# Block-sparse attention before two feed-forward layers: mask added on TensorE, one maximum per four heads, block keys apart

## The chip, the core and the metric

The kernel runs on one core of a Trainium2 chip. The core has five engines with queues of their own: TensorE (PE, matrix products into PSUM), VectorE (DVE), ScalarE (ACT), GpSimd (POOL) and SyncE (SP, which here only issues DMAs). The metric is device time in microseconds (us), the median of several runs.

## The reference

Attention over 2 batches of 8 heads, 768 positions and head size 64, then two feed-forward layers. A query sees the keys less than 16 positions away, and for each block of 32 keys one "block key" (the maximum over the block) and one "block value" (the mean), whose scores get log(32) on top:

```python
k_sum = k.reshape(B, H, nb, block, D).max(axis=3)        # block = 32, nb = 24
v_sum = v.reshape(B, H, nb, block, D).mean(axis=3)
scores_l = scale * np.matmul(q, k.transpose(0, 1, 3, 2)) # scale = 1/8
scores_s = scale * np.einsum('bhsd,bhnd->bhsn', q, k_sum) + np.log(block)
scores_l_m = np.where(mask_l, scores_l, -1000000000.0)   # |i - j| < 16
scores_all = np.concatenate([scores_l_m, scores_s], axis=-1)
a = np.exp(scores_all - np.max(scores_all, axis=-1, keepdims=True))
a = a / (np.sum(a, axis=-1, keepdims=True) + 1e-09)
out = np.matmul(a, np.concatenate([v, v_sum], axis=2))
x = moe(x):  h = x @ w_in;  (h - tanh(h)) @ w_out
y = moe2(x): h = x @ w_in;  (h * tanh(softplus(h))) @ w_out
```

The feed-forward layers have 1536 tokens, width 512 and inner width 2048.

## The kernel before

The attention works in 12 units u of 128 queries, six to a batch (UPB = 6). The eight heads are packed in four pairs hp; the two heads of a pair, e = 0 and 1, lie on partitions 0 to 63 and 64 to 127. The 128 queries of a unit fall in two halves s of T = 64, and a half sees a window of KW = 96 keys and NB = 24 block keys: KA = 120 columns of scores. So a score product uses a quarter (64 by 64) of TensorE's array, and four of them, for the two s and two e, can be in it at once.

For unit u the work is:

- **qk(u)** (L300): 16 float32 products of 120 columns. Each becomes two instructions in the trace. The tile kt of the unit holds the 160 window keys with a copy of the 24 block keys at either end, so that one run of 120 columns is window plus block keys. The results go to two PSUM tiles, "s" for e = 0 and "tr" for e = 1.
- **softmax(u, e)** (L316): for each of the four hp one fused DVE instruction adds the mask (a float32 tile, which also holds the log term), scales by -1/8, writes to the tile aa in SBUF and gives the minimum, which is the negated maximum. Four exponentials on ACT then turn aa into weights, with their sums.
- **norm(u)** (L334): the reciprocal of the sums on DVE, and one multiplication for each e, on POOL or (for the entries in NORM_DVE) on DVE.
- **a_trans(u, e)** (L346): four transposes on TensorE, and a copy asb from PSUM, on DVE for the entries in ASB_DVE and on ACT for the others.
- **av(u)** (L358): the products of weights and values, 32 instructions of 64 columns; then x_hi on ACT and x_lo on DVE (L369, L373) split the result in two for the feed-forward products.

The block keys come from k_sum (L250, a maximum on DVE for each of a batch's six key tiles); k_fill (L260) copies them to both ends of every kt. For the first batch load_k_own (L223) loads each unit's own 128 keys only, and k_edges (L228) copies the 16 edge keys from the neighbours on ACT. v_sum, v_trans and v_fill (L265 to L296) make the block values; v_trans(1) borrows a "tr" tile at step 17.

A loop of steps j (L439) writes the order out. At step j it issues qk(j/2) if j is even, softmax for (j-1), norm(u) at j = 2u+3, a_trans at j = 2u+5 and 2u+6, av at j = 2u+7, x_hi a step later, and then what the table `todo` (L383 to L431) has for that step: loads, k_sum, k_fill, v_sum. Each engine runs its queue in this order. Each PSUM tag has two buffers. From step 19 on, pieces of the feed-forward weights are converted in between (conv_tick), and at steps 24, 25 and 29 the first feed-forward products are put in TensorE's queue (more_in).

## Time and profile before

| | |
|---|---|
| time, median of 3 runs | 604.6 us (602.49 to 605.14) |
| the profiled execution: time, span | 603.07 us, 601.3 us |
| TensorE busy | 578.8 us, 96% of the span, 3212 instructions |
| DVE busy | 417.8 us, 69% |
| ACT busy | 328.5 us, 55% |
| POOL busy | 53.4 us, 9% |

A line of a timeline gives the start and the length in us, the engine, the line of the kernel, the operation, what it writes and reads, and, in brackets, how long the engine was idle just before and which engine's work ended that. The granted clock is 1.00 where TensorE runs at 2.4 GHz and 0.50 at 1.2 GHz.

### The profile page before, as it was taken

How to read it: one execution, taken by the hardware profiler on the slowest of the kernel's cores; microseconds unless marked ns; L12 is line 12 of the kernel's file. 1: busy time of each engine (PE TensorE's matmuls, PEld its weight loads, DVE VectorE, ACT ScalarE, POOL GpSimd, SP SyncE). 2: the span in 40 equal slices, each digit the busy share in tenths (PEclk: the TensorE clock that was granted, in tenths of full speed). 3: DMA queues.
4: the chain of work that ended last, by engine and by line, in shares of the span. 5: the costliest groups of instructions: out<-in, count | busy, mean ns of one | idle time of the engine just before them, and what ended most of it. 6: DMA issues, size and time to landing. Idle time of an engine off the chain costs nothing.

```text
span 601.3 us, 9203 instructions
## 1 busy us (share of the span) xinstructions
PE 578.8 (96%) x3212; PEld 479.0 (80%) x3212; DVE 417.8 (69%) x968; ACT 328.5 (55%) x791; POOL 53.4 (9%) x109
## 2 busy tenths in 40 slices
PE   6768899999999999999999999999999999999997
PEld 5556788888888888888888888888888888888885
DVE  5797978886251222377776489997688777597785
ACT  4788878885251122367765456664464444454442
POOL 6465660000000000000000000000000000000000
PEclk9798899999999999999999999999999999999999
DMA  9997567765020000226661102100100000100001
GB/s 271 257 306 213 154 184 238 222 218 168 0 88 0 1 0 1 62 88 192 197 186 43 40 8 63 52 2 1 55 16 1 1 1 0 71 1 1 1 1 70
DMA packets 32110, 52.20 MB, mean 87 GB/s; under 512 B 3200, under 2 KB 25728, under 8 KB 32064
## 3 DMA queue, kind: packets, MB, share of 16 engines
q1 hardware_dynamic: 32064, 51.62, 28.5%
q8 instruction: 25, 0.41, 0.3%
q14 instruction: 21, 0.17, 0.1%
HBM read 48.07 MB, written 3.15 MB: 85 GB/s over the span
## 4 chain that ended last, share of the span: by engine, by line
PE 88%; DMA 4%; DVE 3%; ACT 2%; SPq 1%; issue 1%; POOL 0%; ACTq 0%
PE aT L478 7%; PE aT L479 7%; PE tr L479 7%; PE x L479 7%; PE aT L480 7%; PE tr L480 7%; PE x L480 7%; PE x L478 7%; PE tr L478 7%; PE s L479 7%; PE s L478 7%; PE s L480 7%; DMA kt<-in_kw_dram 3%; ACT aa L329 1%; DMA vtc<-in_vt_dram 1%; PE x L363 1%
## 5 line engine op out<-in xcount | busy, mean ns | idle before, releaser
L503 DVE TENSOR_TENSOR glo<-t,ghi 128x512 fp32r<-128x512 f32 x48 | 33.4, 695 | 85.4 <-ACT ghi L498 85.4
L498 ACT ACTIVATE ghi<-t 128x512 fp32r<-128x512 f32 x48 | 30.2, 629 | 96.5 <-PE tr L480 96.5
L478 PE MATMUL aT<-xhi,w 128*128 128x512 f32 x192 | 74.9, 390 | 0.0
L478 PE MATMUL s<-xhi,w 128*128 128x512 f32 x192 | 74.9, 390 | 0.0
L480 PE MATMUL s<-xhi,w 128*128 128x512 f32 x192 | 74.7, 389 | 0.0
L480 PE MATMUL aT<-xhi,w 128*128 128x512 f32 x192 | 74.7, 389 | 0.0
L479 PE MATMUL s<-xlo,w 128*128 128x512 f32 x192 | 74.7, 389 | 0.0
L479 PE MATMUL aT<-xlo,w 128*128 128x512 f32 x192 | 74.7, 389 | 0.0
L114 ACT ACTIVATE top<-raw 128x256 f16<-128x256 bf16 x128 | 61.5, 486 | 12.2 <-ACT w L132 4.8
L121 DVE SCALAR_TENSOR_TENSOR cv<-raw,top 128x256 int32<-128x256 int32 x128 | 55.4, 434 | 11.8 <-ACT top L114 7.6
L132 ACT ACTIVATE w<-cv 128x256 fp32r<-128x256 f32 x120 | 47.6, 402 | 10.7 <-DVE cv L121 9.8
L137 DVE TENSOR_TENSOR w<-cv,w 128x256 fp32r<-128x256 f32 x114 | 48.4, 426 | 0.1
L534 DVE SCALAR_TENSOR_TENSOR t<-n,r 128x512 f32<-128x512 f32 x48 | 33.1, 689 | 17.4 <-ACT r L531 17.3
L503 DVE TENSOR_TENSOR glo<-n,ghi 128x512 fp32r<-128x512 f32 x48 | 33.1, 690 | 15.5 <-ACT ghi L498 15.5
L498 ACT ACTIVATE ghi<-n 128x512 fp32r<-128x512 f32 x48 | 30.3, 632 | 24.4 <-PE tr L479 16.1
L329 ACT ACTIVATE aa<-aa,neg 128x120 f32<-128x120 f32 x96 | 36.6, 384 | 12.4 <-DVE neg L324 12.4
L480 PEld LDWEIGHTS aT<-xhi,w 128*128 128x128 f32 x192 | 36.1, 188 | 7.5
L480 PEld LDWEIGHTS s<-xhi,w 128*128 128x128 f32 x192 | 36.1, 188 | 7.5
L478 PEld LDWEIGHTS aT<-xhi,w 128*128 128x128 f32 x192 | 36.0, 188 | 7.5
L478 PEld LDWEIGHTS s<-xhi,w 128*128 128x128 f32 x192 | 36.0, 188 | 7.5
L479 PEld LDWEIGHTS s<-xlo,w 128*128 128x128 f32 x192 | 36.0, 188 | 7.4
L479 PEld LDWEIGHTS aT<-xlo,w 128*128 128x128 f32 x192 | 36.0, 188 | 7.4
(97 smaller groups left out, 1293.1 us busy)
## 6 DMA issues: line engine op xcount, KB each, us to landing
raw<-in_w_dram SPq DMA_DIRECT2D x128, 255.8 KB, 3.6
vu<-in_vw_dram SPq DMA_DIRECT2D x24, 192.0 KB, 4.9
qt<-in_qt_dram SPq DMA_DIRECT2D x12, 256.0 KB, 4.9
vtc<-in_vt_dram SPq DMA_DIRECT2D x6, 512.0 KB, 6.7
out_dram<-o SPq DMA_DIRECT2D x9, 256.0 KB, 2.0
kt<-in_kw_dram SPq DMA_DIRECT2D x6, 320.0 KB, 8.5
kt<-in_kw_dram SPq DMA_DIRECT2D x6, 256.0 KB
out_dram<-t SPq DMA_DIRECT2D x3, 256.0 KB
```

Source lines behind the costliest of these rows:

```text
L114: nc.scalar.activation(out=tops[n % len(tops)].bitcast(F16).rearrange("p (n t) -> p n t", t=2)[:, :, 1], in_=raws[n].bitcast(BF16).rearran ...
L121: nc.vector.scalar_tensor_tensor(out=tmps[n], in0=raws.pop(n).bitcast(I32).rearrange("p (n t) -> p n t", t=2)[:, :, 0], scalar=13, in1=top ...
L132: nc.scalar.activation(out=hi, in_=t, func=ACTF.Copy)
L137: (nc.gpsimd if on_pool else nc.vector).tensor_tensor(out=W[i][:, 1, o:o + PW], in0=tmps.pop(n).bitcast(F32), in1=W[i][:, 0, o:o + PW].bit ...
L329: nc.scalar.activation(out=aa[u][:, e, hp, :], in_=aa[u][:, e, hp, :], func=ACTF.Exp, scale=-1.0, bias=neg[u][:, e, hp:hp + 1], accum_out= ...
L363: nc.tensor.matmul(out=xps[u][64 * e:64 * e + 64, hp, T * s:T * s + T], lhsT=vu[u % 3][:, s, 2 * hp + e, :], rhs=asb[u, e][:, hp, T * s:T ...
L478: nc.tensor.matmul(out=out, lhsT=w[0], rhs=x[0], start=first, stop=False)
L479: nc.tensor.matmul(out=out, lhsT=w[0], rhs=x[1], start=False, stop=False)
L480: nc.tensor.matmul(out=out, lhsT=w[1], rhs=x[0], start=False, stop=last)
L498: nc.scalar.activation(out=ghi, in_=t, func=ACTF.Copy)
L503: nc.vector.tensor_tensor(out=glo, in0=t, in1=ghi.bitcast(F32), op=ALU.subtract)
L534: nc.vector.scalar_tensor_tensor(out=ts[z], in0=ns[z], scalar=2.0, in1=rs[z], op0=ALU.add, op1=ALU.mult)
```

## The change

Four things change in the attention; the feed-forward layers stay.

1. qk(u) first puts the mask into PSUM: four bfloat16 products of an identity with the mask, repeated for the four hp (384 columns), and four of a constant matrix of ones with "logs" (96 columns), three rows of which add up to 8 log(32). Then, for each hp, four float32 products with the window keys (96 columns) and four with the block keys (24 columns) are added on top.
2. max_(u), at the odd step 2u+1, takes the maxima of four heads in one DVE reduction for each e, and one small multiplication makes the negated, scaled maxima of all eight. exps(u, e) reads the scores from PSUM.
3. The block keys stay in their own tensor ksum. k_fill and k_edges go, kt holds the 160 window keys alone, and all key loads bring their edges.
4. The tables for DVE go: norm multiplies on POOL always, a_trans copies on ACT for e = 0 and on DVE for e = 1. The block part of the values lies at the same partitions for both s, so a value load is one DMA and v_fill two.

```diff
-        kt = [kq.tile([128, HP, KU + 2 * NB], F32, name=f"kt{n}") for n in range(NK)]
+        kt = [kq.tile([128, HP, KU], F32, name=f"kt{n}") for n in range(NK)]
...
-        masks = [con.tile([128, KA], F32, name=f"mask{m}") for m in range(3)]
+        masks = [con.tile([128, KW], BF16, name=f"mask{m}") for m in range(3)]
+        logs = con.tile([128, NB], BF16, name="logs")
+        ones = con.tile([128, T], BF16, name="ones")
+        identb = con.tile([128, T], BF16, name="identb")
...
         def load_v(u):
-            for s in range(2):
-                nc.sync.dma_start(out=vu[u % 3][WND[s][0]:WND[s][1], s], in_=vw_d[u, s])
+            nc.sync.dma_start(out=vu[u % 3][NB:KA], in_=vw_d[u].rearrange("s p h d -> p s h d"))
...
-        def k_fill(u):
-            eng = nc.vector if u in FILL_DVE else nc.gpsimd
-            for o in (0, NB + KU):
-                eng.tensor_copy(kt[u % NK][:, :, o:o + NB], ksum[u // UPB])
...
         def qk(u):
+            w, b = u % UPB, u // UPB
             for e in range(2):
                 sc[u, e] = pst(("s", "tr")[e])[:, 0:HP * KA].rearrange("p (a n) -> p a n", a=HP)
-            for hp in range(HP):
+
+            def tiles(reg, lhs, rhs, first=False, last=False):
                 for s in range(2):
                     for e in range(2):
                         d = slice(64 * e, 64 * e + 64)
-                        k0 = s * (NB + T)
                         nc.tensor.matmul(
-                            out=sc[u, e][T * s:T * s + T, hp, :],
-                            lhsT=qt[u % 3][d, hp, T * s:T * s + T],
-                            rhs=kt[u % NK][d, hp, k0:k0 + KA],
+                            out=reg(sc[u, e][T * s:T * s + T]), lhsT=lhs(d, s), rhs=rhs(d, s),
+                            start=first, stop=last,
                         )
...
+            tiles(lambda z: z[:, :, NB:KA], lambda d, s: identb[d], mask, True)
+            tiles(
+                lambda z: z[:, :, 0:NB], lambda d, s: ones[d],
+                lambda d, s: logs[d].unsqueeze(1).to_broadcast([T, HP, NB]),
+            )
+            for hp in range(HP):
+                q = lambda d, s: qt[u % 3][d, hp, T * s:T * s + T]
+                tiles(lambda z: z[:, hp, NB:KA], q, lambda d, s: kt[u % NK][d, hp, T * s:T * s + KW])
+                tiles(lambda z: z[:, hp, 0:NB], q, lambda d, s: ksum[b][d, hp, :], False, hp == HP - 1)
+
+        def max_(u):
+            m = two.tile([128, 2, HP], F32, tag="max", name="max")
+            neg[u] = two.tile([128, 2, HP], F32, tag="neg", name="neg")
+            for e in range(2):
+                nc.vector.tensor_reduce(out=m[:, e], in_=sc[u, e], axis=AX.X, op=ALU.max)
+            nc.vector.tensor_scalar(
+                out=neg[u], in0=m, scalar1=-1.0 / math.sqrt(D), scalar2=None, op0=ALU.mult
+            )
...
-            for hp in range(HP):
-                nc.vector.tensor_tensor_reduce(
-                    out=aa[u][:, e, hp, :], in0=pv[:, hp, :], in1=m, scale=-1.0 / math.sqrt(D),
-                    scalar=3.0e38, op0=ALU.add, op1=ALU.min, accum_out=neg[u][:, e, hp:hp + 1],
-                )
             for hp in range(HP):
                 nc.scalar.activation(
-                    out=aa[u][:, e, hp, :], in_=aa[u][:, e, hp, :], func=ACTF.Exp,
-                    scale=-1.0, bias=neg[u][:, e, hp:hp + 1], accum_out=sums[u][:, e, hp:hp + 1],
+                    out=aa[u][:, e, hp, :], in_=pv[:, hp, :], func=ACTF.Exp,
+                    scale=1.0 / math.sqrt(D), bias=neg[u][:, e, hp:hp + 1],
+                    accum_out=sums[u][:, e, hp:hp + 1],
                 )
...
-                (nc.vector if 2 * u + e in NORM_DVE else nc.gpsimd).tensor_tensor(
+                nc.gpsimd.tensor_tensor(
...
-            if 2 * u + e in ASB_DVE:
+            if e:
                 nc.vector.tensor_copy(t, pv)
...
         for u in range(UPB):
-            load_k_own(u)
+            load_k(u)
...
+            if j < NJ and j % 2 == 1:
+                max_(j // 2)
             if 1 <= j <= NJ:
-                softmax(*divmod(j - 1, 2))
+                exps(*divmod(j - 1, 2))
```

**TensorE, the scores of unit 3 and what stands behind them.** Before (s_393 and tr_394 are the two score tiles, kt3 and qt0 the keys and queries, aT the transposes of unit 0, x the products with its values):

```order
L310 MATMUL s_393<-kt3_92,qt0_97 64x120
L310 MATMUL tr_394<-kt3_92,qt0_97 64x120
...
L349 MATMUL aT_419<-ident_106,aa_257 120x128 x4
L349 MATMUL aT_443<-ident_106,aa_300 120x128 x4
L363 MATMUL x_450<-asb_375,vu0_100 64x64
L363 MATMUL x_450<-asb_424,vu0_100 64x64
```

Now:

```order
L301 LDWEIGHTS identb_108
L301 MATMUL s_453<-mask1_104,identb_108 64x4x96
...
L301 LDWEIGHTS ones_107
L301 MATMUL s_453<-logs_106,ones_107 64x4x24
...
L301 MATMUL s_453<-kt3_92,qt0_97 64x96
...
L301 MATMUL s_453<-ksum_226,qt0_97 64x24
...
L356 MATMUL aT_499<-ident_109,aa_286 120x128 x4
L356 MATMUL aT_523<-ident_109,aa_347 120x128 x4
L370 MATMUL x_530<-asb_437,vu0_100 64x64
```

The 16 products of the unit have become 32 narrower ones, with eight bfloat16 products ahead of them; the transposes and the value products behind them are the same.

**DVE, from unit 8 to unit 9.** Before (rd: sums and reciprocals of unit 7, asb: copies of transposes, L324: the fused instruction with the row that stores its minimum, of unit 8 and then, from s_924, of unit 9):

```order
L336 TENSOR_SCALAR rd_877<-sums_782 128x8
L339 RECIPROCAL rd_877<-rd_877 128x8
L375 TENSOR_TENSOR xlo1_71<-x_804,xhi1_68 128x4x128
L353 COPY asb_888<-aT_883 120x512
L324 ISA aa_866,neg_867<-tr_833,mask1_104 128x120
L324 ISA neg_867 128x1
...
L353 COPY asb_955<-aT_950 120x512
L324 ISA aa_957,neg_958<-s_924,mask1_104 128x120
```

Now (max_1139 and neg_1140 are of unit 9, rd_1044 of unit 7, rd_1150 of unit 8):

```order
L343 TENSOR_SCALAR rd_1044<-sums_936 128x8
L346 RECIPROCAL rd_1044<-rd_1044 128x8
L382 TENSOR_TENSOR xlo1_71<-x_954,xhi1_68 128x4x128
L360 COPY asb_1137<-aT_1132 120x512
L324 TENSOR_REDUCE max_1139<-s_1086 128x4
L324 TENSOR_REDUCE max_1139<-tr_1087 128x4
L325 TENSOR_SCALAR neg_1140<-max_1139 128x8
L343 TENSOR_SCALAR rd_1150<-sums_1039 128x8
```

The maxima of both e of a unit now stand together, behind the copy asb that stood ahead of e = 0 alone, and one of the two copies has moved to ACT.

**ACT at the same place.** Before (aa_866 is unit 8, aa_957 unit 9, vu0 the transposed block values of v_trans(1)):

```order
L329 ACTIVATE aa_866,sums_868<-aa_866,neg_867 128x120 x4
L287 ACTIVATE vu0_100<-tr_890 24x512 x2
L371 ACTIVATE xhi1_68<-x_897 128x4x128
L329 ACTIVATE aa_866,sums_868<-aa_866,neg_867 128x120 x4
L329 ACTIVATE aa_957,sums_959<-aa_957,neg_958 128x120 x4
```

Now (aa_1038 is unit 8, aa_1144 unit 9):

```order
L335 ACTIVATE aa_1038,sums_1039<-s_979,neg_1034 128x120 x4
L362 ACTIVATE asb_1055<-aT_1050 120x512
L279 ACTIVATE vu0_100<-tr_1057 24x512 x2
L378 ACTIVATE xhi1_68<-x_1064 128x4x128
L335 ACTIVATE aa_1038,sums_1039<-tr_980,neg_1034 128x120 x4
L335 ACTIVATE aa_1144,sums_1145<-s_1086,neg_1140 128x120 x4
```

A copy of a transpose has come between the first four exponentials and vu, and the exponentials read the score tiles s and tr.

## Rows read from the trace of the kernel before

**Rows 1.** The page: busy time by engine, and shares of the last chain.

```profile
PE 578.8 (96%) x3212; PEld 479.0 (80%) x3212; DVE 417.8 (69%) x968; ACT 328.5 (55%) x791; POOL 53.4 (9%) x109
...
PE 88%; DMA 4%; DVE 3%; ACT 2%; SPq 1%; issue 1%; POOL 0%; ACTq 0%
```

**Rows 2.** Timeline of TensorE: start, length, work, idle time before.

```profile
62.11 1.15 PE L363 MATMUL x<-asb,vu 120*64 120x64 f32 x30 [1.65 <-DVE asb L353]
...
76.76 0.62 PE L349 MATMUL aT<-ident,aa 128*120 128x128 f32 x4 [0.16 <-POOL aa L341]
```

**Rows 3.** Timeline of ACT: first exponentials of units 2, 3, 5, 8, 9, 10.

```profile
19.18 0.40 ACT L329 ACTIVATE aa<-aa,neg 128x120 f32<-128x120 f32 x1 [0.38 <-DVE neg L324]
...
26.45 0.39 ACT L329 ACTIVATE aa<-aa,neg 128x120 f32<-128x120 f32 x1
...
35.86 0.39 ACT L329 ACTIVATE aa<-aa,neg 128x120 f32<-128x120 f32 x1 [0.86 <-DVE neg L324]
...
51.88 0.40 ACT L329 ACTIVATE aa<-aa,neg 128x120 f32<-128x120 f32 x1 [1.79 <-DVE neg L324]
...
57.31 0.40 ACT L329 ACTIVATE aa<-aa,neg 128x120 f32<-128x120 f32 x1 [0.59 <-DVE neg L324]
...
62.40 0.38 ACT L329 ACTIVATE aa<-aa,neg 128x120 f32<-128x120 f32 x1
```

**Rows 4.** Timeline of all engines at the start, unit 0.

```profile
8.79 0.69 DVE L255 TENSOR_REDUCE ksum<-kt 128x16 f32<-128x512 f32 x1 [0.18 <-DMA kt<-in_kw_dram]
...
9.82 0.28 PE L310 MATMUL s<-kt,qt 64*64 64x120 f32 x1 [2.31 <-DVE kt L263]
...
11.14 0.28 DVE L324 CUSTOM_DVE_ANT_0 aa<-s,mask 128x120 f32<-128x120 f32 x1 [0.59 <-PE tr L310]
...
11.47 0.40 ACT L329 ACTIVATE aa<-aa,neg 128x120 f32<-128x120 f32 x1 [2.44 <-DVE neg L324]
...
12.77 0.68 DVE L272 TENSOR_REDUCE vsum<-vtc 128x16 f32<-128x512 f32 x1
...
12.99 0.38 ACT L329 ACTIVATE aa<-aa,neg 128x120 f32<-128x120 f32 x1
```

**Rows 5.** A stretch (its last columns: clock, DMA share, GB/s), and POOL's timeline.

```profile
10.00:20.00 10.00, 6.54 (x102) 5.03 (x99) 8.31 (x55) 7.20 (x37) 6.10 (x15) 0.66 1.05 300
...
11.13 1.97 POOL L276 TENSOR_TENSOR vtc<-vtc 128x256 f32<-128x256 f32 x4 [2.94 <-DMA vtc<-in_vt_dram]
...
17.76 1.98 POOL L276 TENSOR_TENSOR vtc<-vtc 128x256 f32<-128x256 f32 x4 [0.56 <-DMA vtc<-in_vt_dram]
```

**Rows 6.** Timeline of DVE: two reductions in a row, one k_fill.

```profile
17.67 1.28 DVE L272 TENSOR_REDUCE vsum<-vtc 128x16 f32<-128x512 f32 x2
...
42.53 1.11 DVE L263 COPY kt<-ksum 128x96 f32<-128x96 f32 x2
```

**Rows 7.** Groups by form, 0 to 115 us: total busy us, mean ns of one.

```profile
L371 ACT ACTIVATE xhi<-x 128x512 fp32r<-128x512 f32 x12 | 7.0, 583 | 1.6 <-PE x L363 1.6
L498 ACT ACTIVATE ghi<-t 128x512 fp32r<-128x512 f32 x6 | 3.7, 617 | 0.0
```

**Rows 8.** Timeline of TensorE: scores, transposes, value products.

```profile
27.68 0.31 PE L310 MATMUL s<-kt,qt 64*64 64x120 f32 x1
...
28.66 1.09 PE L349 MATMUL aT<-ident,aa 128*120 128x128 f32 x8
...
30.59 1.15 PE L363 MATMUL x<-asb,vu 120*64 120x64 f32 x30 [0.58 <-ACT asb L355]
```

**Rows 9.** Timeline where v_trans(1) stands.

```profile
53.41 1.18 ACT L287 ACTIVATE vu<-tr 24x512 f32<-24x512 f32 x2
...
54.65 0.31 PE L310 MATMUL tr<-kt,qt 64*64 64x120 f32 x1 [1.18 <-ACT vu L287]
```

**Rows 10.** A normalising pair on POOL; TensorE's busy time and clock in a stretch.

```profile
58.30 1.94 POOL L341 TENSOR_TENSOR aa<-aa,rd 128x480 f32<-128x480 f32 x2 [3.06 <-PE x L363]
...
63.50:64.00 0.50, 0.50 (x18) 0.50 0.18 33
```

More of the change, by code (lines that the diff above doesn't have):

```diff
@@ L196, in constants @@
             make_identity(nc, ident)
-            k_edges(0)
+            for e in range(2):
+                h = slice(64 * e, 64 * e + 64)
+                nc.gpsimd.tensor_copy(identb[h], ident[h, h])
+            nc.gpsimd.memset(ones, 1.0)
+            nc.gpsimd.memset(logs, 0.0)
+            left = float(np.float32(math.sqrt(D) * math.log(BLK)))
+            for r in range(3):
+                part = float(np.float32(left).astype(mybir.dt.np(BF16)))
+                left -= part
+                for e in range(2):
+                    nc.gpsimd.affine_select(
+                        out=logs, in_=logs, pattern=[[0, NB]], base=-(64 * e + r), channel_multiplier=1,
+                        compare_op=ALU.not_equal, fill=part,
+                    )
+            assert left == 0.0
             for m in range(3):
                 nc.gpsimd.memset(masks[m], 0.0)
-                for s in range(2):
-                    rows = masks[m][T * s:T * s + T]
-                    nc.gpsimd.memset(rows[:, SUM[s][0]:SUM[s][1]], math.sqrt(D) * math.log(BLK))
-                    reg = rows[:, WND[s][0]:WND[s][1]]
+                for e in range(2):
+                    reg = masks[m][T * e:T * e + T]
                     conds = [([[1, KW]], -1, -1), ([[-1, KW]], 2 * WIN - 1, 1)]
-                    if (m, s) == (0, 0):
+                    if m == 0:
                         conds.append(([[1, KW]], -WIN, 0))
-                    if (m, s) == (2, 1):
+                    if m == 2:
                         conds.append(([[-1, KW]], KW - WIN - 1, 0))
@@ L253, in k_sum @@
                 ksum[b] = two.tile([128, HP, NB], F32, tag="ksum", name="ksum")
-            own = kt[u % NK][:, :, NB + WIN:NB + WIN + 128]
+            own = kt[u % NK][:, :, WIN:WIN + 128]
             nc.vector.tensor_reduce(
@@ L287, in v_trans @@
                 nc.scalar.activation(
-                    out=vu[0][SUM[s][0]:SUM[s][1], s].rearrange("p h d -> p (h d)"), in_=p[0:NB, :],
+                    out=vu[0][0:NB, s].rearrange("p h d -> p (h d)"), in_=p[0:NB, :],
                     func=ACTF.Copy, scale=1.0 / BLK,
@@ L292, in v_fill @@
         def v_fill(n):
[L293 to L296 removed]
+            nc.sync.dma_start(out=vu[n][0:NB], in_=vu[0][0:NB])
         sums, neg, aa, asb, xps, sc = {}, {}, {}, {}, {}, {}
         def qk(u):
+            w, b = u % UPB, u // UPB
             for e in range(2):
                 sc[u, e] = pst(("s", "tr")[e])[:, 0:HP * KA].rearrange("p (a n) -> p a n", a=HP)
[L305 removed]
+            def tiles(reg, lhs, rhs, first=False, last=False):
                 for s in range(2):
@@ new lines, in tiles, with mask @@
+                            start=first, stop=last,
+                        )
+            def mask(d, s):
+                m = masks[0 if (w, s) == (0, 0) else 2 if (w, s) == (UPB - 1, 1) else 1]
+                return m[d].unsqueeze(1).to_broadcast([T, HP, KW])
+            tiles(lambda z: z[:, :, NB:KA], lambda d, s: identb[d], mask, True)
[3 more added lines that the diff above has]
+            )
@@ L400, in attention @@
             k_sum(u)
-            if u:
-                k_edges(u)
-        for u in range(UPB):
-            if u == 0:
-                v_sum(0, 0, 1, True)
-            k_fill(u)
+        v_sum(0, 0, 1, True)
         for u in range(3, NU):
@@ L429, in attention @@
         at(17, L(v_fill, 1), L(v_fill, 2))
-        for u in range(7, 12):
-            at(2 * u - 3, L(k_fill, u))
         NJ = 2 * NU
```

37 lines of the change are left out of this document (7 added, 30 removed).

## The prediction

> **What bounds the kernel now.** The page comes first: TensorE is busy for 96% of the span and holds 88% of the chain that ended last [rows 1]. A share is an average over stages, so the next view is TensorE's own waits. At 62.11 us it has waited 1.65 us for a copy on DVE, and from there to the end its only visible wait is one of 0.16 us at 76.76 [rows 2]. Whatever the attention stage gains or loses before the products av(7) at 62.11 moves the end one for one, and so does work added to TensorE after it; the two feed-forward layers do the same work in both kernels. The question is when av(7) starts.
>
> Before that no single engine is the bound. I follow the first exponentials of each unit (128 queries) on ACT: units 5 and 10 begin theirs at 35.86 and 62.40, so a unit takes 26.54 / 5 = 5.31 us [rows 3]. TensorE's own share of a unit is about 0.98 us of scores, 1.09 of transposes and 1.15 of products with the values [rows 8], 3.2 us. The rest is waiting in a ring: scores, maxima on DVE, exponentials on ACT, normalising on POOL, transposes, copies.
>
> **Start.** The first six key blocks now come with their edges, 320 KB each instead of 256, so 384 KB more stand ahead of everything. In the window 10 to 20 us the queue moves 300 GB/s and the DMA share is full [rows 5]: 1.3 us later. The low end is 0, if whole rows of 2.5 KB move faster than 512-byte pieces; no row shows that, so I take 1.3. The ten edge copies on ACT go and free nothing here, since ACT waits then. The new constants lie on POOL, which is idle for 2.94 us before its first sum [rows 5]; they cost nothing as long as they take no more than that on top of what is there, and their excess if they do. On SP the value loads and the fills of vu are half as many; the keys of the second batch stand behind them there, so this can only help, and I count nothing. The last block's maximum starts at 8.79 us [rows 4]; 1.3 later, and with the maxima below, unit 0's exponentials fall behind 11.47 by some 2.4 us. Part of that is absorbed: unit 2's maxima stand behind the value sums on DVE, whose last input lands at 17.76 [rows 5], then at 19.05. From there one block sum 0.7, maxima 1.4 and 0.1 of waiting give 21.2 us for unit 2's exponentials, against 19.18 [rows 3].
>
> **Scores on TensorE.** Today 32 instructions of 120 columns take 27.68 to 28.66, 0.98 us, 31 ns each with four quarter arrays at work [rows 8]. The change replaces them with 32 of 96 columns, by columns 0.78 us, 32 of 24 columns, and eight bfloat16 products of 384 and 96 columns. The 24-column ones cost 0.20 us by columns. Their high end is the pace of the value products, 30 of 64 columns in 1.15 us on two half arrays [rows 8], 38 ns each, 1.2 us; halved, because four quarters work at once, it is 0.6. I take 0.4, the middle of 0.20 and 0.6. No row shows a bfloat16 product: four of 384 columns and four of 96 at today's rate per column make 0.49 us, the low end is 0 if TensorE does them while it waits for keys or queries, and I take 0.25. Together 1.43 us, with ends 0.98 and 2.5. The Trainium skill, TensorEngine Tiling (Array Packing), section Instruction Overhead, speaks against the split: it says that a matmul has some 60 cycles of overhead and that one column takes as long as sixty. By that rule the 24-column products would cost 0.49 us at 60 columns each instead of 0.4, a pass 1.52 us, and the end 0.5 us more, 606.3 us; no row here has so narrow a product, so the trace neither agrees nor disagrees.
>
> **Maxima on DVE.** What goes: eight fused mask-and-minimum instructions, 11.14 to 12.77, 1.63 us a unit [rows 4], but the first of them released ACT after 0.33 us. Also the copies of the block keys into kt, about 1.1 us for a unit's pair beside busy POOL [rows 6]. What comes: two reductions of 480 elements and one small multiplication. Two reductions of 512 take 1.28 us [rows 6]; from PSUM I take 1.2 for both and 0.2 for the rest, 1.4 us (ends 1.3 and 1.6). So DVE's work falls, but all eight exponentials of a unit wait for the whole 1.4 us. From start of scores to first exponential the path was 9.82 to 11.47, 1.65 us [rows 4]; it becomes 1.43, 0.25 for the last product's own time, and 1.4: 3.1 us.
>
> **Exponentials.** Four take 11.47 to 12.99, 1.52 us [rows 4]. They now read PSUM; a 512-wide ACT copy costs 583 ns from there and 617 from SBUF [rows 7], so 34 ns less each, 1.4 us for four (ends 1.25 and 1.55).
>
> **The new ring.** The score tiles stay in PSUM until ACT has read them; so far DVE freed them. Scores of unit u+2 wait for the last exponentials of unit u. On TensorE's queue a transpose stands behind those scores; on DVE the copy of that transpose stands ahead of the maxima. Two units therefore take: scores 1.7 with the last product, transpose 0.55, copy 0.7, maxima 1.4, then on ACT 1.4, copy 0.5, x_hi 0.5, 1.4. That is 8.15 us, 8.75 with a block sum in DVE's queue: 4.1 to 4.4 a unit. I take 4.3 against 5.31.
>
> **Where v_trans stands** the ring breaks. There the scores wait for ACT to read the transposed sums out of the same pair of tiles: today vu at 53.41 lasts 1.18 us, scores follow at 54.65 [rows 9], and unit 8 to unit 9 takes 51.88 to 57.31, 5.43 us [rows 3]. The change puts a transpose copy, 0.5, before vu on ACT: 1.4 + 0.5 + 1.2 + 1.7 + 0.55 + 0.7 + 1.4 = 7.45 us. At unit 2 to 3 the same, with a block sum and some slow clock, is 8.2 us, against 7.27 [rows 3]; the key blocks then land no later than they are asked for.
>
> **The sum.** First exponentials: unit 2 at 21.2, unit 3 at 29.4, unit 5 two rings later at 38.0 (35.86, so 2.1 late), unit 8 at 50.9 (51.88, 1.0 early), unit 9 at 58.4 (57.31, 1.1 late), unit 10 at 63.1 with a weight conversion of 0.4 (62.40, 0.7 late). av(7) came 0.3 us ahead of that last time; now the maxima lie between, so it comes 1.4 ahead: 61.7, 0.4 early. After it, unit 11's scores cost 0.45 more, and normalising the last two units stands whole on POOL, 1.94 us for two halves [rows 10], about 1.0 us of it more than now and all counted. The copies of the transposes alternate (12 on ACT, 12 on DVE, where it was 13 and 11), which the ring's terms hold. The granted clock was half in 63.5 to 64 [rows 10], behind the wait of 1.65 us; a shorter wait could spare up to 1.7 us there, and the longer one at unit 9 could cost as much, so I put 0. In all -0.4 + 0.45 + 1.0 = +1.1 us. The profiled execution took 603.07 us, 1.8 more than its span of 601.3; the median is 604.6. On the median: 605.7, say 605.8 us.
>
> **Rivals.** (a) Faster: columns alone set TensorE's pace, scores 0.98 us. That takes 0.45 from each of two v_trans steps and from unit 11, 0.22 from each of the six ring steps between units 3 and 10, 2.7 us; the half clock goes too, 1.7. 605.8 - 4.4 = 601.4. For it: today's scores keep four quarters busy at 31 ns. Against it: the value products keep 38 ns at half the columns. (b) Slower: narrow products do not overlap four at a time and the scores take 2.5 us: 1.07 more in two v_trans steps and unit 11, 0.53 in six ring steps, 6.4 us: 612.2. It decides from about 1.75 us a pass, where the loss passes 3 us. (c) The change does not do what it says: DVE gets free time, but ACT's waits for it stay, since the eight exponentials hang on one instruction. Then a unit keeps 5.3 us, the six ring steps give nothing, 6.0 us lost: 611.8. Against it: the second four exponentials need no further wait.
>
> **How the numbers follow.** About 0.5% (3 us) is what a measurement of this kernel can tell from no change. The forecast, a small loss within that, has 0.46; (a) has 0.20; (b) and (c) together 0.34. The low end 601.0 takes (a) in; the high end 612.0 stops just short of (b) and (c), and leaves out what may lie beyond.
>
> **What would show it.** Unit 2 at about 21 us, units apart by 4.3 where 5.31 stood, 7 us or more from unit 8 to unit 9, score passes of 1.4 us, and no TensorE wait worth naming after av(7). A pass of 1.0 or of 2 us, or unit 9's first exponentials before 57 us, would prove the sum wrong.

## The result, and the profile of the changed kernel

The changed kernel takes 608.13 us (median of 9 runs, 606.36 to 610.59), the kernel before 603.29 us in the same session (9 runs, 601.87 to 605.14): 1.0083 times as long, with a 95% interval of 1.0061 to 1.0104. That is 4.8 us more where 1.2 were forecast (605.8 on 604.6), inside the range, but four times the size, and past the 0.5% that can be told from no change.

The profiled execution of the changed kernel is the longest of the nine: 610.59 us, with a span of 608.8, against 603.07 and 601.3 before. Its trace shows 7.5 us of loss, 2.7 more than the medians. The page, which answers [rows 1]:

```profile
PE 585.1 (96%) x3692; PEld 486.2 (80%) x3692; DVE 407.9 (67%) x791; ACT 322.3 (53%) x780; POOL 55.8 (9%) x111
...
PE 89%; DVE 4%; ACT 3%; DMA 1%; issue 1%; POOL 0%; SPq 0%; ACTq 0%
```

DVE and ACT have less to do, as the change intended, and TensorE has 480 products more, with as many weight loads. The shares say nothing about where the time went. The timeline of ACT does: the first exponentials of units 2, 3, 5, 8, 9 and 10, which answer [rows 3].

```profile
21.54 0.36 ACT L335 ACTIVATE aa<-s,neg 128x120 f32<-128x120 f32 x1 [1.57 <-DVE rd L343]
...
30.98 0.36 ACT L335 ACTIVATE aa<-s,neg 128x120 f32<-128x120 f32 x1 [5.22 <-DVE rd L343]
...
39.72 0.36 ACT L335 ACTIVATE aa<-s,neg 128x120 f32<-128x120 f32 x1 [0.26 <-DVE neg L325]
...
56.33 0.36 ACT L335 ACTIVATE aa<-s,neg 128x120 f32<-128x120 f32 x1 [2.98 <-DVE rd L343]
...
65.19 0.36 ACT L335 ACTIVATE aa<-s,neg 128x120 f32<-128x120 f32 x1 [4.15 <-DVE rd L343]
...
70.05 0.36 ACT L335 ACTIVATE aa<-s,neg 128x120 f32<-128x120 f32 x1 [0.37 <-DVE rd L343]
```

| step, us | before | forecast | changed kernel | over forecast |
|---|---|---|---|---|
| start to unit 2 | 19.18 | 21.2 | 21.54 | 0.3 |
| unit 2 to 3 (v_trans) | 7.27 | 8.2 | 9.44 | 1.2 |
| units 3 to 5 | 9.41 | 8.6 | 8.74 | 0.1 |
| units 5 to 8 | 16.02 | 12.9 | 16.61 | 3.7 |
| unit 8 to 9 (v_trans) | 5.43 | 7.45 | 8.86 | 1.4 |
| unit 9 to 10 | 5.09 | 4.7 | 4.86 | 0.2 |

The six excesses make 6.9 us: unit 10 at 70.05 where 63.1 was forecast. On TensorE the main part of av(7), which answers the first of [rows 2], starts 6.5 us late:

```profile
68.65 1.15 PE L370 MATMUL x<-asb,vu 120*64 120x64 f32 x30 [0.47 <-DVE asb L360]
```

The end is 7.5 us late, so what lies behind av(7) costs 1.0 us (1.45 forecast). What the forecast missed lies before av(7), mostly in two places: from unit 5 to unit 8, and in the two steps with v_trans. Against the kernel before, units 5 to 8 lose only 0.6 us; what is missing there is the 3.1 us that were to be gained, which should have paid for the start and the v_trans steps.

**Units 5 to 8.** The timeline of TensorE stops twice in the middle of a score pass:

```profile
43.98 0.24 PE L301 MATMUL tr<-ksum,qt 64*64 64x24 f32 x2
45.62 0.18 PE L301 MATMUL s<-ksum,qt 64*64 64x24 f32 x1 [1.39 <-issue]
...
49.89 0.24 PE L301 MATMUL s<-ksum,qt 64*64 64x24 f32 x2
52.11 0.18 PE L301 MATMUL tr<-ksum,qt 64*64 64x24 f32 x1 [1.97 <-issue]
```

"issue" means that nothing in the profile held the engine. All that these products need was there: their neighbours of the same pass, with the same keys and queries, had run. The kernel before has no such wait. That leaves the instructions themselves. They come by DMA queues of their own; TensorE's, by its packets, in the kernel before and in the changed one:

```profile
q8 instruction: 25, 0.41, 0.3%
```

```profile
q8 instruction: 29, 0.48, 0.3%
```

TensorE's 2 x 3692 products and weight loads over 29 packets are 255 to a packet, 2 x 3212 over 25 are 257: the queue brings pages of some 256 instructions. The trace also has each of these packets, 16384 bytes long, with its time: one runs from 42.96 to 44.30 and the next from 49.42 to 50.69, and the two waits end 1.3 and 1.4 us behind their ends. With the few semaphore instructions of TensorE's queue counted, it stops after 1473 and after 1729 instructions of the program: 256 apart.

A unit had 144 of them (64 for the scores, 16 for the transposes, 64 for the products with values); now it has 224. One page lasted 1.8 units, some 9 us; now it lasts 1.1, under 5 us in a ring of 4.3. Meanwhile the DMA engines are full with loads: a share of 1.02 in both of these stretches, in which TensorE does next to nothing (columns as in [rows 5]). That a page stands behind the loads is the theory to test.

```profile
44.00:45.50 1.50, 0.22 (x11) 0.12 (x4) 1.21 (x3) 1.50 (x9) 1.42 (x4) 1.00 1.02 386
50.00:52.00 2.00, 0.13 (x6) 0.03 (x1) 0.28 (x1) 2.00 (x9) 2.00 (x3) 1.00 1.02 197
```

**The v_trans steps.** TensorE waits for vu longer than in the kernel before, where it was 1.12 us (at 21.94) and 1.18:

```profile
24.47 0.48 PE L301 MATMUL tr<-mask,identb 64*64 64x384 bf16 x1 [1.79 <-ACT vu L279]
...
59.27 0.48 PE L301 MATMUL tr<-mask,identb 64*64 64x384 bf16 x1 [2.58 <-ACT vu L279]
```

Behind these waits the granted clock is half:

```profile
24.50:27.00 2.50, 2.50 (x71) 2.50 (x70) 0.00 (x0) 1.27 (x8) 0.00 (x0) 0.50 0.41 109
...
59.50:61.50 2.00, 2.00 (x65) 2.00 (x61) 0.00 (x0) 1.54 (x9) 0.00 (x0) 0.50 0.52 131
```

The pass from 59.27 takes 2.7 us where one at full clock takes 1.5, and the eight transposes behind it 1.96 instead of 1.09. The kernel before is not free of this: its eight transposes at 23.43 took 1.96 us as well, and over 10 to 75 us the mean granted clock is 0.87 in both traces. So the half clock is a cost against the forecast, which had these steps at nearly full clock; over the whole attention these two traces have the same share of it.

**At the start** a third thing was not foreseen. Without the edge copies, ACT's first work is an exponential, and the load of its table, which ran at 0.73 before anything was needed, now stands right ahead of it:

```profile
13.07 1.28 ACT L335 ACT_TABLE_LOAD   x1 [13.07 <-DVE neg L325]
14.37 0.36 ACT L335 ACTIVATE aa<-s,neg 128x120 f32<-128x120 f32 x1
```

### The profile page after: what moved, and what is told of

Its sections match the earlier page's. It is cut to its first block, busy times and chain, and to the rows that moved or that the text cites. A ratio compares the mean times of both kernels' runs of the same rounds, so it can differ in the third digit from the quotient of the medians.

```text
span 608.8 us, 9955 instructions
## 1 busy us (share of the span) xinstructions
PE 585.1 (96%) x3692; PEld 486.2 (80%) x3692; DVE 407.9 (67%) x791; ACT 322.3 (53%) x780; POOL 55.8 (9%) x111
## 4 chain that ended last, share of the span: by engine, by line
PE 89%; DVE 4%; ACT 3%; DMA 1%; issue 1%; POOL 0%; SPq 0%; ACTq 0%
PE aT L480 7%; PE x L480 7%; PE tr L480 7%; PE aT L482 7%; PE aT L481 7%; PE tr L482 7%; PE x L482 7%; PE x L481 7%; PE tr L481 7%; PE s L480 7%; PE s L482 7%; PE s L481 7%; ACT aa L335 2%; DVE max L324 2%; PE s L301 1%; PE aT L356 1%
## 5 line engine op out<-in xcount | busy, mean ns | idle before, releaser
L521 ACT ACTIVATE t<-aT 128x512 f32<-128x512 f32 x24 | 14.4, 599 | 44.2 <-PE aT L482 30.7
```

Of the source, the lines that this page charges most:

```text
L521: nc.scalar.activation(out=t, in_=hs[z], func=ACTF.Exp)
```

## The experiments

The theory: the narrow products make TensorE run out of instructions while the DMA engines are full ("fetch"), and the steps with v_trans lose time to the half clock behind the longer waits for vu. The rivals: the waits come from the products themselves or from PSUM; the table load or the wait of all eight exponentials is what counts. Ratios are to the kernel before, run beside each; the interval of the changed kernel itself is 1.0061 to 1.0104. e1_table and e2_merged lie above it, e7_before_more and e13_fill_act below; the times of the others cannot be told from it, and there the traces decide, each of one execution.

### The table load: e1_table and e5_table64

```diff
     nc.gpsimd.memset(two_c, 2.0)
+    early = big.tile([128, 1], F32, name="early")
+    nc.scalar.activation(out=early, in_=two_c, func=ACTF.Exp)
```

> One tiny exponential on ACT is put ahead of everything, so that the table load (1.28 us at 13.07 in the changed kernel, right ahead of unit 0's first exponential) happens while ACT is idle. If that load lies on the path that sets the end, unit 0's exponentials start at 13.0 instead of 14.37, unit 2's at 20.3 to 20.6 instead of 21.54, and the time falls by 0.6 to 1.3 us, to about 607.0. If the value sums or the loads bound unit 2 anyway, unit 2 moves by less than 0.4 us and the time stays within 0.3 us of 608.1.

619.19 us, ratio 1.0262 (1.0240 to 1.0284): 11 us more instead of 1 less. The load did move to 0.73 and unit 0 to 13.01. But in the stretch 120 to 600 us, far from the edit, fewer products fit (the number behind TensorE's busy time). The same stretch of e1_table, then of e5_table64:

```profile
120.00:600.00 480.00, 480.00 (x2077) 389.87 (x2077) 317.63 (x598) 235.20 (x468) 0.56 (x2) 1.00 0.17 51
```

```profile
120.00:600.00 480.00, 480.00 (x2119) 397.59 (x2118) 323.37 (x606) 237.90 (x469) 0.56 (x2) 1.00 0.16 50
```

e5_table64 differs in one number, `big.tile([128, 64], ...)[:, 0:1]`.

> The early exponential of e1_table again, but its result takes the first column of a tile of 64 columns (256 bytes) instead of a tile of 1 column, so that the tiles allocated behind it (weights, activations) move by 256 bytes and not by 4. If e1_table lost its 11 us because the products of the feed-forward layers read tiles that are shifted by 4 bytes (395 ns each instead of 389), they are back at 389 ns here and the time is 606.5 to 607.8: 608.1 less what the table load costs on the path. If the early exponential itself is to blame, the time stays near 619.

608.77 us, ratio 1.0080 (1.0052 to 1.0108). So the 11 us of e1_table came from the 4 bytes by which its tile moved all tiles behind it. With 256 bytes the products are back at full pace; in the trace unit 0's exponentials start at 12.71 and unit 2's at 20.18, 1.36 us earlier than in the changed kernel. Unit 5 keeps this gain (38.35, 1.37 earlier), and the span of the trace is 605.6, 3.2 us shorter; the medians of eight and nine executions show nothing of it (608.77 and 608.13). So the table load is on the path of the first units, but no gain from taking it away can be seen in the time.

### Fewer instructions with wider weights: e2_merged

```diff
-                tiles(lambda z: z[:, hp, 0:NB], q, lambda d, s: ksum[b][d, hp, :], False, hp == HP - 1)
+                both(
+                    lambda z: z[:, hp, 0:NB], lambda d: qt[u % 3][d, hp, :],
+                    lambda d: ksum[b][d, hp, :], False, hp == HP - 1,
+                )
```

(`both` makes one product for e = 0 and one for e = 1, with 128 columns of weights; logs and inner masks likewise. A pass of the inner units has 104 instructions, not the 100 of the expectation.)

> The products with the block keys, with logs and (in the eight inner units) with the mask are made for both halves of a unit by one instruction with 128 columns of weights: a score pass has 100 instructions (weight loads and products) instead of 144. Theory 'fetch': TensorE stands still at 43.98 and 49.89, in the middle of a pass, because it has run through a page of 256 instructions before the next page came in. With 40 instructions less in a unit both waits vanish, unit 6 to unit 8 takes 9 to 10 us instead of 12.5, and the time falls by 3 to 5 us, to 603 to 605. Rival 'something else holds a pass up in its middle' (PSUM, the products of the block keys themselves): waits of 1 to 2 us within a pass stay, and only the shorter pass is gained, 0.1 to 0.3 us a step: 606.5 to 608.

626.41 us, ratio 1.0382 (1.0362 to 1.0402). The waits in the middle of passes are gone (one wait for instructions is left, 0.73 us at 63.16, between transposes), but a pass now takes 3.08 us at full clock (41.85 to 44.93) instead of 1.44. TensorE's timeline, one group of keys and one of block keys, and the next (first and last of each):

```profile
42.28 0.29 PE L302 MATMUL s<-kt,qt 64*64 64x96 f32 x1
...
42.61 0.29 PE L314 MATMUL s<-ksum,qt 64*128 64x24 f32 x1
...
42.75 0.27 PE L314 MATMUL tr<-ksum,qt 64*128 64x24 f32 x1
42.95 0.29 PE L302 MATMUL s<-kt,qt 64*64 64x96 f32 x1
```

Four instructions of 24 columns take 0.34 us of the queue (42.61 to 42.95), as much as eight of 96 (0.33): a group of one form (64 by 64) does not overlap with one of the other (64 by 128). The Trainium skill, TensorEngine Tiling (Array Packing), section Key Properties, says that a change of the tiling mode drains TensorE; this trace agrees, 0.33 us per group, eight times in a pass. The run answers its question only half: instructions were saved, but at a slower pace a page lasts longer anyway.

### More instructions in the kernel before: e7_before_more

```diff
+            for n in range(20):
+                for e in range(2):
+                    d = slice(64 * e, 64 * e + 64)
+                    nc.tensor.matmul(out=sc[u, e][0:T, 0, 0:1], lhsT=tiny[d, 0:T], rhs=tiny[d, 0:1])
             for hp in range(HP):
```

> The kernel before, with 40 bfloat16 products of one column (80 instructions with their weight loads) put ahead of the scores of each unit on TensorE; the scores then overwrite their result. Theory 'fetch': with 80 instructions more a unit runs through about a page, as in the changed kernel, and waits that the trace cannot put down to another engine, 0.5 to 2 us long and some 256 instructions apart, appear on TensorE between 35 and 60 us, where the kernel before has none. Rival 'the waits come from the products of the block keys or from the mask': no such wait here; the time grows only by what the tiny products take, 0.5 to 1.5 us in a pass.

605.71 us, ratio 1.0037 (1.0014 to 1.0059), and the waits appear, four of them, in a kernel that had none:

```profile
17.52 0.36 PE L316 MATMUL s<-kt,qt 64*64 64x120 f32 x1 [1.47 <-issue]
...
37.46 0.16 PE L310 MATMUL s<-tiny 64*64 64x1 bf16 x1 [0.75 <-issue]
...
43.67 0.16 PE L310 MATMUL s<-tiny 64*64 64x1 bf16 x1 [1.50 <-issue]
...
49.90 0.16 PE L310 MATMUL s<-tiny 64*64 64x1 bf16 x1 [0.60 <-issue]
```

The last three come 2, 16 and 30 tiny products into a unit's pass: each time 14 products, 28 instructions, further on, and a unit has 224; 252 from one wait to the next, and 256, a page, with the four semaphore instructions in between. From 37.46 to 43.67 and to 49.90 are 6.2 us each. The rival falls: neither mask nor block keys are needed for such a wait, only the count. The place in the program says the same: in the eleven traces of this document that have such waits, 23 in all, TensorE stops each time 193 or 194 instructions behind a multiple of 256, whatever product stands there, and goes on 1.3 to 1.8 us after the end of a packet of its instruction queue.

### Fewer transfers: e3_raw_late and e11_quiet

```diff
-        at(12, L(v_sum, 1, 0, 1, True), L(conv_ahead, n_raw))
+        at(12, L(v_sum, 1, 0, 1, True))
...
-        at(16, L(v_sum, 1, 2, 1))
+        at(16, L(v_sum, 1, 2, 1), L(conv_ahead, n_raw))
```

> The first loads of raw weights, six of 256 KB, are issued at step 16 instead of step 12; nothing else changes. Theory 'the page of instructions stands behind the data in the DMA engines': in 43 to 53 us there is less to move, the waits of 1.39 and 1.97 us in the middle of passes shrink to under half or vanish, and the time falls by 1 to 3 us, to 605 to 607. Rival 'a page takes the same time whatever else moves': both waits stay at 1.4 and 2 us, and the time is 608 or, as the weights then come late, more.

607.16 us, ratio 1.0055 (1.0034 to 1.0076). The two waits are 0.62 and 1.43 us, and a third one of 1.15 us has come at 63.53, where the late loads now run (DMA share 0.64 in 62 to 64, where the changed kernel has 0.00). The waits go where the transfers go, but their sum stays (3.20 us; 3.36 in the changed kernel).

e11_quiet moves these loads to step 18 and leaves the three loads of the second batch's values for v_sum out:

```diff
         def load_vt(b, g):
+            if b:
+                vtc[b, g] = vtc[0, g]
+                return
```

> The changed kernel with less to transfer: the three loads of 512 KB for the second batch's block values are left out (its block values are summed from the first batch's tiles, which takes the same time), and the first raw weights are issued at step 18 instead of 12. The instructions of TensorE are the same. Theory 'a page of instructions stands behind the data': with the DMA engines no longer full in 40 to 53 us, the waits of 1.39 and 1.97 us in the middle of the passes vanish, units 5 to 8 follow at 4.1 to 4.8 us, and the time falls by 3 us or more, to 605 or less. Rival 'a page needs its 5 to 6 us anyway': both waits stay, and the time falls by no more than 1 us.

606.40 us, ratio 1.0052 (1.0035 to 1.0068). No wait in the middle of a pass is left before 67 us. First exponentials of units 5, 8 and 9, and the stretch ahead of the first wait, whose DMA share was 1.02 in the changed kernel:

```profile
39.28 0.36 ACT L338 ACTIVATE aa<-s,neg 128x120 f32<-128x120 f32 x1 [0.96 <-DVE rd L346]
...
51.97 0.36 ACT L338 ACTIVATE aa<-s,neg 128x120 f32<-128x120 f32 x1 [0.64 <-DVE rd L346]
...
59.17 0.36 ACT L338 ACTIVATE aa<-s,neg 128x120 f32<-128x120 f32 x1 [2.49 <-DVE rd L346]
```

```profile
42.00:44.00 2.00, 2.00 (x78) 1.91 (x81) 1.56 (x5) 2.00 (x14) 1.69 (x6) 1.00 0.03 10
```

Units 5 to 8 take 12.69 us, where 12.9 were forecast and 16.61 measured, with the same instructions on TensorE. That settles fetch: it is the transfers that a page stands behind. The packets show how. In the changed kernel those that ended the two waits began 3.4 and 3.8 us after TensorE had entered the page before (at 39.57 and 45.62); here the packets for the same two pages began 0.8 and 0.6 us after it (at 38.56 and 43.55).

The time fell by 1.7 us, less than the 3 expected, and the intervals of the two kernels overlap. The trace shows more, a span of 603.0, 5.8 us shorter, of which 1.7 are unit 8 to 9, at full clock here (7.20 us); a little is given back behind unit 9, where the late weights fill the DMA engines again (share 1.01 to 1.05 from 64 to 68 us): unit 9 to 10 takes 5.25 us, and TensorE waits 1.03 us for instructions at 67.33. But this trace is of the shortest of twelve executions and the changed kernel's of the longest of nine, so for the time the medians count.

### The clock: e4_warm

```diff
+            if u in (3, 9):
+                for n in range(3):
+                    nc.tensor.matmul(
+                        out=sc[u, 0][0:T], lhsT=ident[0:64, 0:T], rhs=kt[u % NK][0:64, :, 0:KA],
+                        start=True, stop=True,
+                    )
```

> Ahead of the scores of units 3 and 9, three float32 products of 480 columns are put on TensorE, whose result is overwritten by the mask; they fill the time in which TensorE waits for vu. Theory 'clock': the passes of these units took 2.70 us at half clock behind waits of 1.79 and 2.58 us, and the eight transposes behind them 1.96 us; at full clock they take 1.5 and 1.1 us, units 3 and 9 begin their exponentials 1.5 to 2.5 us earlier each, and the time falls by 2 to 4 us, to 604 to 606. Rival 'these passes are slow for another reason': they stay at 2.7 us and the time is 608 to 609, since the three products stand ahead of the scores.

606.37 us, ratio 1.0077 (1.0051 to 1.0104). In the trace the theory holds: the clock is full in both stretches, and the transposes take 1.09 us again. One wait for instructions is left, 1.88 us at 49.10.

```profile
24.50:26.00 1.50, 1.50 (x73) 1.32 (x65) 0.47 (x1) 1.13 (x8) 0.00 (x0) 1.00 0.82 293
56.00:58.00 2.00, 1.86 (x74) 1.55 (x72) 0.00 (x0) 2.00 (x10) 0.00 (x0) 1.00 0.74 185
```

Unit 2 to 3 takes 8.09 us (21.41 to 29.50) and unit 8 to 9 7.20 (53.48 to 60.68), where the prediction had 8.2 (with some slow clock) and 7.45: at full clock its two steps were right. e3_raw_late says the same of unit 9 without such products. There the clock stayed full behind the same wait for vu, and unit 8 to 9 took 7.19 us:

```profile
57.02 0.32 PE L301 MATMUL tr<-mask,identb 64*64 64x384 bf16 x1 [2.58 <-ACT vu L279]
```

So the half clock is what these steps lose, but it does not follow every such wait. Nor do the three products seem to prevent it in every execution: the mean granted clock of a whole execution was 0.992 to 0.997 in six of the eleven (605.06 to 606.37 us) and 0.983 to 0.989 in the other five (609.53 to 612.08). The median is 1.8 us lower than the changed kernel's, but the interval does not tell the two apart.

### The wait of all eight exponentials: e6_neg

```diff
             for e in range(2):
                 nc.vector.tensor_reduce(out=m[:, e], in_=sc[u, e], axis=AX.X, op=ALU.max)
-            nc.vector.tensor_scalar(out=neg[u], in0=m, ...)
+                nc.vector.tensor_scalar(out=neg[u][:, e], in0=m[:, e], ...)
```

> The multiplication that negates the maxima is split, one for each e right behind its reduction, so that the first four exponentials wait for one reduction (0.62 us and 0.17) and not for two. If the wait of all eight on 1.4 us of DVE lies on the path, as the prediction counted it, units 2, 3 and 9 each come about 0.5 us earlier, and so do most ring steps: the time falls by 1.5 to 3 us, to 605 to 606.5. If pages of instructions and the clock bound the attention, the steps between units 5 and 8 keep their length and the time falls by less than 1 us.

607.08 us, ratio 1.0054 (1.0032 to 1.0075): a gain of 1 us at most, not told apart. Units 2, 3 and 5 start 1.0, 2.4 and 2.7 us earlier (20.52, 28.59, 37.00), and units 5 to 8 take 15.6 us, with waits of 1.2 and 1.7 us for instructions. In this trace the gain is kept: unit 9 comes 4.6 us earlier and the end 3.5. As the changed kernel's trace is 2.5 us above its median and this one at its own, the medians count, and they leave 1.0 us, within their noise.

### The causes together: e10_all and e12_one_warm

```diff
-                nc.scalar.activation(out=vu[0][0:NB, s]..., in_=p[0:NB, :], func=ACTF.Copy, scale=1.0 / BLK)
+                nc.vector.tensor_scalar(out=vu[0][0:NB, s]..., in0=p[0:NB, :], scalar1=1.0 / BLK, ...)
...
+        for j in range(6):
+            at(13 + j, L(conv_ahead, j + 1))
```

(with the edits of e4_warm, two products, and of e6_neg)

> Four edits together: the negation split (e6_neg), two products ahead of the scores of units 3 and 9 that keep TensorE busy (e4_warm), the copies vu of v_trans on DVE, which is idle there, instead of behind a transpose copy on ACT, and the first raw weights issued one at a time at steps 13 to 18. If the causes found so far add up (clock 1.8 us, wait of all eight exponentials 1.0, vu about 0.8 in each of two steps, late raw loads 1.0), the time is 602 to 603.5, level with the kernel before, with 6 to 6.5 us from unit 8 to unit 9. If they overlap, because a page of instructions bounds units 5 to 8 whatever comes ahead of it, it stays at 604.5 to 606.

608.56 us, ratio 1.0085 (1.0055 to 1.0115): nothing gained. TensorE still waits 0.62 and 1.77 us for instructions (44.44 and 50.67), and units 5 to 8 take 15.12 us. Ahead of unit 3 the two products themselves ran at half clock (0.93 to 1.00 us an instruction, 0.44 in e4_warm) and held the scores up: unit 3 at 30.94.

> e10_all without its two products ahead of unit 3, which there ran at half clock themselves and held a quarter of the array until 25.20 while vu was done at 23.14; those ahead of unit 9 stay. If these products cost e10_all what the causes had given, unit 3 begins its exponentials at 28 to 29 us instead of 30.94, the feed-forward products begin about 2 us earlier than at 71.04, and the time is 604 to 606. If pages of instructions and the clock give the time back, it stays at 606.5 to 608.5.

607.76 us, ratio 1.0078 (1.0050 to 1.0105). Unit 3 comes at 28.11, 2.9 us earlier than in the changed kernel, and unit 5 at 36.28, 3.4 earlier. Then:

```profile
36.28 0.36 ACT L342 ACTIVATE aa<-s,neg 128x120 f32<-128x120 f32 x1 [0.39 <-DVE neg L332]
...
55.13 0.36 ACT L342 ACTIVATE aa<-s,neg 128x120 f32<-128x120 f32 x1 [1.34 <-DVE neg L332]
```

```profile
37.29 0.23 PE L301 MATMUL s<-logs,ones 64*64 64x96 bf16 x1 [0.96 <-issue]
...
45.30 0.30 PE L301 MATMUL s<-ksum,qt 64*64 64x24 f32 x1 [3.46 <-issue]
```

18.85 us for three units. What came earlier waits for its page here: 8.0 us from the end of one such wait to the end of the next, with a third of 0.96 us at 64.70. Of the 3.4 us, 1.2 are left at unit 8: in this trace the gain of the other edits is seen to go.

### Fewer instructions with the same form: e9_keys_before and e13_fill_act

e9_keys_before takes back the third part of the change: block keys at both ends of kt, one product of 120 columns.

```diff
-                tiles(lambda z: z[:, hp, NB:KA], q, lambda d, s: kt[u % NK][d, hp, T * s:T * s + KW])
-                tiles(lambda z: z[:, hp, 0:NB], q, lambda d, s: ksum[b][d, hp, :], False, hp == HP - 1)
+                tiles(
+                    lambda z, s: z[:, hp, :], q,
+                    lambda d, s: kt[u % NK][d, hp, s * (NB + T):s * (NB + T) + KA], False, hp == HP - 1,
+                )
```

> The changed kernel with its third part undone: the block keys are copied into the key tiles again, the first six blocks come without their edges, and the keys take one product of 120 columns in place of 96 and 24; the mask on TensorE, the maxima of four heads and the multiplications on POOL stay. A pass has 80 instructions instead of 144. Theory 'fetch and clock': no wait in the middle of a pass, a pass of about 1.2 us, units 3 to 8 follow at 4.3 to 4.8 us, the table load is back at the start, and the time is 600 to 604; the two steps with v_trans still run at half clock. Rival 'the copies of the block keys on DVE cost as much as the split': units at 5 us and more, and a time of 605 to 608.

606.57 us, ratio 1.0056 (1.0031 to 1.0082). No wait for instructions is left (26 packets), and a pass takes 1.17 us. But units 5 to 8 take 15.33 us (39.79 to 55.12): DVE's copies of the block keys stand ahead of the maxima, as its timeline shows.

```profile
40.68 0.68 DVE L290 TENSOR_REDUCE vsum<-vtc 128x16 f32<-128x512 f32 x1
41.28 1.57 DVE L281 COPY kt<-ksum 128x96 f32<-128x96 f32 x2
42.77 0.68 DVE L391 COPY asb<-aT 120x512 f32<-120x512 f32 x1
43.37 0.64 DVE L355 TENSOR_REDUCE max<-s 128x4 f32<-128x480 f32 x1
```

They are not the only cause: the granted clock was half from 44 to 47 us, and the pass from 45.08 took 2.2 us.

e13_fill_act puts those copies of the second batch on ACT, vu on DVE, and splits the negation:

```diff
-                eng.tensor_copy(kt[u % NK][:, :, o:o + NB], ksum[u // UPB])
+                if u < UPB:
+                    eng = nc.vector if u in FILL_DVE else nc.gpsimd
+                    eng.tensor_copy(kt[u % NK][:, :, o:o + NB], ksum[u // UPB])
+                else:
+                    nc.scalar.copy(kt[u % NK][:, :, o:o + NB], ksum[u // UPB])
```

> e9_keys_before (keys of 120 columns again, no wait for instructions) with three edits: the negation split, the copies vu on DVE, and the copies of the block keys of the second batch on ACT (0.5 us a unit) instead of DVE, where they took 0.5 to 1.6 us ahead of the maxima. If DVE's queue is what kept e9_keys_before at 5.0 to 5.2 us a unit, units 5 to 8 follow at 4.3 to 4.7 us, unit 9 comes 6 to 7 us behind unit 8, and the time is 601.5 to 604, level with the kernel before or better. If the copies lengthen ACT's part of the ring by as much as they free on DVE, units stay at 5 us and the time at 604.5 to 606.

602.65 us, and 602.65 us for the kernel before beside it: ratio 1.000 (0.998 to 1.002). Units 5, 8 and 9:

```profile
37.34 0.36 ACT L369 ACTIVATE aa<-s,neg 128x120 f32<-128x120 f32 x1 [0.41 <-DVE neg L359]
...
50.03 0.36 ACT L369 ACTIVATE aa<-s,neg 128x120 f32<-128x120 f32 x1 [0.39 <-DVE neg L359]
...
57.42 0.36 ACT L369 ACTIVATE aa<-s,neg 128x120 f32<-128x120 f32 x1 [1.52 <-DVE neg L359]
```

12.69 us for the three units, 4.23 each, the ring of the forecast (units 3 to 5 take 10.17). So with the third part of the change undone, and with it fewer instructions, shorter first loads and the early table load, and with these three edits, the whole loss is regained. Nothing is gained beyond it: the v_trans step still takes 7.39 us (5.43 before), and in it TensorE waits 2.52 us for POOL's value sum. How much each of these did was not separated. No version beat the kernel before.

## Why the prediction was right, and where it was wrong

The sign and the range held, the size did not: 4.8 us where 1.2 were forecast. The outcome that was given 0.46 was a loss within 3 us; the measured one lies between it and the rivals (b) and (c), by a mechanism that none of the three names. (The high end of 612.0 does not stop short of (c), as the text says: its 611.8 lies inside.) Of the working, this held and this did not.

- **Bound.** Right: behind av(7) the loss hardly changes (6.5 us there, 7.5 at the end).
- **Start.** Right in the sum by luck, wrong in the parts: unit 2 at 21.54 for 21.2. The value sums on DVE, which were to set it, were done at 19.40; the maxima of unit 2 waited until 20.01 for the scores, and these for unit 0's exponentials (1.80 and 1.05 us, until 17.27). The last block's maximum ends at 10.07, 0.6 later than in [rows 4] where 1.3 were put, and the table load adds 1.28 that was overlooked: that the removed edge copies "free nothing" left out that they held the table load at the start. What it is worth at the end stays open (e5_table64).
- **Scores.** Right: from the start of a pass to the transposes behind it are 1.44, 1.43 and 1.44 us (transposes at 32.21, 66.70 and 71.17) and twice 1.57 (36.30 and 40.95), for 1.43. By e9_keys_before's 1.17 the bfloat16 products cost 0.19 (0.25 forecast) and the split 0.27 (0.20). The 1.52 us by the Trainium skill's TensorEngine Tiling (Array Packing), section Instruction Overhead, lie between these passes: the trace does not decide against it. By that estimate the split alone costs 0.29 (0.49 less the 0.20 that the longer products lose in columns), and the 0.27 measured agree.
- **Maxima and exponentials.** Right: 1.26 us for two reductions and 0.17 for the negation (20.01 to 21.44; 1.4 forecast), 1.39 for four exponentials (1.4).
- **The new ring.** Right as long as instructions are there: 4.37 us a unit from 3 to 5, 4.23 in e11_quiet and in e13_fill_act, for 4.3. **This is the step that failed:** from unit 5 on the ring was taken to be bound by engines alone. The sum counted the columns of 80 instructions more in a unit, not their delivery. A page every 6 us or so, with the DMA engines full, turned 12.9 us into 16.6 in the profiled execution and took the whole gain of the ring. Six other traces with nearly the same instructions and loads (e1, e3, e4, e5, e6, e10) have 15.05 to 15.59 there and so keep 0.4 to 1.0 us of it; e12_one_warm has 18.85.
- **v_trans steps.** Mechanism right, a term put at nothing: at full clock they take 8.09 and 7.20 us (8.2 and 7.45 forecast). The prediction saw that the longer wait at unit 9 could cost up to 1.7 us of clock and set it against what a shorter wait before av(7) would spare; the steps lost 1.35 us (9.44) and 1.66 (8.86) against e4_warm, and behind av(7) only 0.45 less than forecast was lost. Of the 1.4 us by which the second wait grew, the copy put ahead of vu takes 0.48; the rest was not taken apart.
- **Behind av(7).** 1.0 us for 1.45. But TensorE waits 0.34, 0.42 and 0.50 us there (until 72.17, 73.47 and 81.97), where the prediction's signs had "no TensorE wait worth naming".
- **Rivals.** (a) and (b) fell with the pass of 1.44 us, which is neither 0.98 nor 2.5; nor did the half clock go, as (a) had it. (c) came near units 5 to 8 for a wrong reason: they took 5.5 us each, but for their instructions, and e11_quiet, in which the eight exponentials wait as before, has 4.23.

That the median lost only 4.8 us where the profiled run lost 7.5 fits waits that differ from run to run: 1.39 and 1.97 us in the changed kernel, 0.6 and 1.2 in e5_table64, 3.46 in e12_one_warm. The clock does not explain it: an execution of the same mean granted clock as the profiled one (0.985 and 0.986) took 607.38 us. That the waits make up the difference is argued, not shown: each kernel has one trace. How the 4.8 us of the median divide among start, pages and v_trans steps stays open too.

## What to carry to other kernels

Count instructions as a cost of their own: packets of the engine's instruction queue over its instructions give the page, and a page must last longer than it takes to come through DMA engines that are full (6.0 to 6.5 us here, and 8.0 once). A wait put down to "issue" in the middle of a run of like products, about a page after the last such wait, is this one; making the rest faster can make it longer (e12_one_warm). And a longer wait of TensorE should be priced with a half clock behind it, in the pass and the transposes that follow, as one of two outcomes: behind the same 2.58 us it came in the changed kernel and not in e3_raw_late. Last, a trace is one execution: its time should be set beside the median of its kernel before a gain read from it is believed.

## What was not expected of the hardware

- **Instructions come late.** With a DMA share of 0.99 to 1.08, TensorE got a page of 256 instructions every 6.2 us (e7_before_more; 6.5 in the changed kernel, 8.0 in e12_one_warm); with a share between 0.03 and 0.88 (e11_quiet, 40 to 52 us) it did not wait. The Trainium skill, Runtime: NRT & Kernel Launch, section Instruction fetch mechanics, says that instructions come in blocks of 256 and that the fetch is mostly hidden. The block agrees with the waits 256 instructions apart here; hidden it is not, when the blocks stand behind loads.
- **The form of the products.** Groups of 64 by 64 and of 64 by 128 do not overlap: 0.33 us for each group, a pass of 3.08 us instead of 1.44 with 104 instructions instead of 144 (e2_merged).
- **Four bytes.** Tiles moved by 4 bytes made the products of the feed-forward layers 2% slower (2077 instead of 2119 in 480 us; 395 ns each instead of 389) and cost 10 us (e1_table against e5_table64). Which tile's place counts was not tried.
